# Counting in a routing round: 18 matmuls into [threshold, expert] in place of three with block-diagonal extraction

## The chip, the cores and the metric

The kernel runs on one core of a Trainium2 chip. The metric is the device time of one execution, in microseconds. The profile is that of one execution and comes with its own time.

## What is computed

Three steps follow each other. Attention with queries averaged in pairs gives 2304 rows of 512. A dense layer without a nonlinearity, `((x @ w1) * (x @ w2)) @ w3 @ w_out`, gives new rows of the same shape. Then a mixture of eight experts gives each token to one expert, at most 288 tokens to an expert, in the order of the logits:

```python
    cap = N // E
    logits = x @ w_gate
    order = np.argsort(-logits.flatten())
    for idx in order:
        tok, e = (int(idx) // E, int(idx) % E)
        if assigned[tok] >= 0 or counts[e] >= cap:
            continue
        assigned[tok] = e
        counts[e] += 1
    ...
    for e in range(E):
        mask = assigned == e
        h = np.maximum(x[mask] @ w1[e], 0.0)
        out[mask] = h @ w2[e]
```

## The kernel before

The program is written as a list of operations with costs, dependences and priorities. A planner (`Sched`) simulates the engines with these costs and writes the instructions out in the order of its planned start times. So each engine has one fixed queue in which the stages are interleaved, and the costs that the code states for an operation decide where it stands. Matrix products in float32 are made of three passes, high by high, high by low and low by high part.

The stages in time are: attention (to about 510 us); the hidden layer h, with the logits computed from folded weights beside it (to about 770 us); the product of w3 and w_out, called W, and then x2, the rows that the experts read (to about 953 us); the eight experts (to the end). Routing needs only the logits. Its operations have a smaller priority number than those of W, x2 and the experts, so the planner takes them first where they are ready, and fills the gaps in TensorE's queue with the matmuls of these stages.

Routing replaces the greedy loop by eight phases. Seven of them fix one expert each. In a phase every token that is still free goes to its best open expert (`rt_oh`, one-hot), with its largest logit (`rt_mu`). Then eight rounds search the threshold, four bits at a time, at which the first expert becomes full. A round is a serial chain:

- VectorE compares the logits of 128 x 18 tokens with 15 candidate thresholds (`rt_mask`, [128, 18, 15]).
- TensorE counts in three matmuls of six token groups each, 90 weight columns by 48 moving columns. Only the blocks on the diagonal, where the group of the mask equals the group of the one-hot, mean something.
- VectorE multiplies by a block-diagonal mask (`rt_cnt`), adds the six groups up (`rt_sum`), and spreads the sums over 15 thresholds by 8 experts (`rt_own`, 90 rows of the tile `own8`). A 97th row of `own8` holds minus the free places, `rem`, written once a phase.
- TensorE sums the rows of `own8` with a matrix of ones, so that each partition gets count minus free places.
- VectorE takes the maximum over experts (`rt_any`), compares with zero (`rt_flag`), adds the flags up (`rt_n`), and makes the next base and thresholds of it (`rt_base`, `rt_thr`, `rt_G`).

After the eight rounds a phase assigns its tokens (`rt_ge`, `rt_rows`, a matmul with `rc_neg` and `rc_tri`, `rt_inc` and others). `pick` names the expert that is full, which starts its weight loads by GpSimd's queue, and `slot_lists` makes the list of its tokens with 18 small matmuls (`sl_oh`, `sl_mv`), after which GpSimd gathers their rows. Expert number n can begin when list n is there and x2 is written.

PSUM tiles for routing, the transposes of the gathered rows (`g`) and of the experts' outputs (`ey`) come from the same four slots (`s_pt`). Most operations of these stages are issued through one helper, so the profile gives them all the line L113, and they are told apart by tile. In the rows, u, uh and ul are an expert's weights and their parts, xh, xl and exh, exl the gathered tokens, ehh and ehl the hidden values.

Of the kernel before, what the change touches and what calls it, by code (L numbers as in the profile page):

```python
# [11 lines left out]
F32 = mybir.dt.float32  # L12
F32R = mybir.dt.float32r
BF16 = mybir.dt.bfloat16
F16 = mybir.dt.float16
# [756 lines left out]
NCG = 6  # L772
# [3 lines left out]
def routing_consts(nc, pool, spare):  # L776
# [35 lines left out]

    v = tmp([NCG * NTHR, NCG, 8], F32)
    nc.gpsimd.iota(v, pattern=[[-NTHR, NCG], [0, 8]], base=0, channel_multiplier=1, allow_small_or_imprecise_dtypes=True)
    own = tmp([NCG * NTHR, NCG, 8], F32)
    nc.vector.tensor_scalar(own, v, NTHR - 0.5, None, op0=OP.is_lt)
    c["own"] = diag = pool.tile([NCG * NTHR, NCG, 8], BF16, name="rc_diag")
    nc.vector.scalar_tensor_tensor(diag, v, 0.0, own, op0=OP.is_ge, op1=OP.mult)
    u = tmp([NCG * NTHR, NTHR, NCG], F32)
    nc.gpsimd.iota(u, pattern=[[-1, NTHR], [-NTHR, NCG]], base=0, channel_multiplier=1, allow_small_or_imprecise_dtypes=True)  # L820
    nc.vector.tensor_scalar(u, u, 0.0, None, op0=OP.is_equal)
    c["thr"] = sel = pool.tile([NCG * NTHR, NTHR], F16, name="rc_thr")
    with nc.allow_low_precision(reason="0 or 1"):
        nc.vector.tensor_reduce(sel, u, axis=AX.X, op=OP.max)
    c["ones16"] = ones16 = pool.tile([97, 128], F16, name="rc_ones16")
    nc.vector.memset(ones16, 1.0)

# [25 lines left out]
def routing(nc, sch, rp, slots, c, L, keyL, A, rows_of, idx, prio, prio_l):  # L853
# [11 lines left out]
    r_mx, r_mask = ring("mx", 1, [128, NC], F32), ring("mask", 2, [128, NC, NTHR], BF16)  # L865
    r_flag, r_any, r_n = ring("flag", 2, [128, NTHR], F32), ring("any", 2, [128, NTHR], F32), ring("n", 2, [128, 1], I32)
    r_cnt, r_sum = ring("cnt", 2, [NCG * NTHR, NCG, 8], F16), ring("sum", 2, [NCG * NTHR, 8], F16)
    own8 = rp.tile([97, NTHR, 8], F16, name="rt_own8")
# [17 lines left out]
    dve(120, lambda: nc.vector.memset(own8, 0.0), [], ["own8", "own8r"])  # L886
# [15 lines left out]
    for ph in range(8):  # L902
# [18 lines left out]
        if ph < 7:  # L921

            dve(120, lambda: nc.vector.tensor_scalar(
                own8[96:97], rem[96:97, None, :].to_broadcast([1, NTHR, 8]), 4096.0, -1.0, op0=OP.min, op1=OP.mult), [keyR], ["own8r"])
            base = kb = None
            for rd, b in enumerate(BITS):
# [4 lines left out]
                else:  # L931
# [11 lines left out]
                dve(NC * T, lambda mask=mask, thr=thr, T=T, mu=mu: nc.vector.tensor_tensor(  # L943
                    mask[:, :, :T], mu[:, :, None].to_broadcast([128, NC, T]),
                    thr[:, None, :T].bitcast(F32).to_broadcast([128, NC, T]), op=OP.is_ge), [kmu, kth], [kma])
                ps = Hold(slots)

                def f(ps=ps, mask=mask, oh=oh):
                    for g in range(NC // NCG):
                        gs = slice(g * NCG, g * NCG + NCG)  # L950
                        nc.tensor.matmul(ps.tile[0:NCG * NTHR, 0:NCG * 8], mask[:, gs, :].rearrange("p a t -> p (a t)"),
                                         oh[:, gs, :].rearrange("p a e -> p (a e)"), start=(g == 0), stop=(g == NC // NCG - 1))
                sch.op("PE", 200, f, r=[kma, koh], takes=ps, prio=prio, slack=RT_SLACK)
                (cnt, kc), (sm, ksm), (flag, kf), (any_, kany), (n, kn) = r_cnt(), r_sum(), r_flag(), r_any(), r_n()
                dve(NCG * 8, lambda ps=ps, cnt=cnt: nc.vector.tensor_tensor(
                    cnt.rearrange("p a e -> p (a e)"), ps.tile[0:NCG * NTHR, 0:NCG * 8], c["own"].rearrange("p a e -> p (a e)"), op=OP.mult),
                    [], [kc], uses=[ps])

                def f(cnt=cnt, sm=sm):
                    with nc.allow_low_precision(reason="counts up to 384 are exact"):  # L960
                        nc.vector.tensor_reduce(sm, cnt.rearrange("p a e -> p e a"), axis=AX.X, op=OP.add)
                dve(NCG * 8, f, [kc], [ksm])
                dve(NTHR * 8, lambda sm=sm: nc.vector.tensor_tensor(
                    own8[0:NCG * NTHR], sm[:, None, :].to_broadcast([NCG * NTHR, NTHR, 8]),
                    c["thr"][:, :, None].to_broadcast([NCG * NTHR, NTHR, 8]), op=OP.mult), [ksm], ["own8"])
                ps = Hold(slots)
                sch.op("PE", 110, lambda ps=ps: nc.tensor.matmul(
                    ps.tile[:, 0:NTHR * 8], c["ones16"], own8.rearrange("p t e -> p (t e)"), start=True, stop=True), r=["own8", "own8r"],
                    takes=ps, prio=prio, slack=RT_SLACK)
                dve(NTHR * 8, lambda ps=ps, any_=any_: nc.vector.tensor_reduce(  # L970
                    any_, ps.tile[:, 0:NTHR * 8].rearrange("p (t e) -> p t e", e=8), axis=AX.X, op=OP.max), [], [kany], uses=[ps])
                dve(NTHR, lambda any_=any_, flag=flag: nc.vector.tensor_scalar(flag, any_, 0.0, None, op0=OP.is_ge), [kany], [kf])

                def f(flag=flag, n=n):
# [798 lines left out]
```

## Time and profile before

| | |
|---|---|
| median of three runs | 1259.6 us (1254.34 to 1266.79) |
| the profiled execution | 1264.11 us, of which the span 1262.3 us |
| mean granted TensorE clock | 0.972 |
| TensorE busy | 1175.4 us (93%) |
| VectorE busy | 1037.6 us (82%) |
| GpSimd busy | 692.0 us (55%) |
| ScalarE busy | 640.4 us (51%) |

The span runs from the first to the last instruction. The clock is the share of full speed that TensorE was granted. In rows of groups, the form `out<-in` gives tiles without buffer numbers; the idle time is that of the engine just before these instructions, with what ended it. PE is TensorE, PEld its weight loads, DVE VectorE, ACT ScalarE, POOL GpSimd.

### The profile page before, as it was taken

What the parts mean: (1) busy time and instruction counts of PE and PEld (TensorE: products, weight loads), DVE (VectorE), ACT (ScalarE), POOL (GpSimd) and SP (SyncE); (2) the same over time, 40 slices, a digit from 0 to 9 for tenths busy, and PEclk for the clock granted to TensorE, in tenths of its full rate; (3) what the DMA queues carried; (4) which work ended last, traced back from release to release, by engine and by line L of the source; (5) the groups of instructions that cost most, each with busy time, mean ns of one, the idle gap of its engine ahead of it and who ended that gap; (6) DMA issues with size and microseconds to landing.
All of it is one profiled execution on the core that took longest, in us unless ns stands there. A gap on an engine that the chain in (4) does not pass through costs nothing.

```text
span 1262.3 us, 24072 instructions
## 1 busy us (share of the span) xinstructions
PE 1175.4 (93%) x8377; PEld 1107.6 (88%) x8377; DVE 1037.6 (82%) x2958; ACT 640.4 (51%) x1333; POOL 692.0 (55%) x710
## 2 busy tenths in 40 slices
PE   7999999999999999899999999978898898889995
PEld 5999999999999999899999997756678888789895
DVE  7998999999999999988777876778777998888641
ACT  6888888888888888333222202122222433443330
POOL 4566666666666755455322443264444787767740
PEclk9999999999999999899999999999998999898898
DMA  8676666667666441244555523432223454444530
GB/s 203 157 177 136 156 154 159 153 150 156 153 161 157 115 100 54 68 162 175 174 167 172 180 68 118 158 92 51 63 55 116 158 162 150 148 158 124 186 120 19
DMA packets 116617, 169.87 MB, mean 135 GB/s; under 512 B 47959, under 2 KB 79710, under 8 KB 116494
## 3 DMA queue, kind: packets, MB, share of 16 engines
q1 hardware_dynamic: 104110, 125.33, 38.6%
q0 software_dynamic: 12384, 43.00, 10.5%
q8 instruction: 66, 1.08, 0.4%
q14 instruction: 57, 0.47, 0.1%
HBM read 104.87 MB, written 24.45 MB: 102 GB/s over the span
## 4 chain that ended last, share of the span: by engine, by line
PE 71%; DVE 20%; DMA 3%; issue 2%; POOL 2%; SPq 1%; ACT 1%; POOLq 0%; DVEq 0%; ACTq 0%
PE pb L113 30%; PE s L590 12%; PE pt L614 7%; PE pt L113 6%; PE pt L664 6%; PE s L664 5%; PE s L614 3%; DVE cv_v L113 2%; DVE rt_own L113 2%; DVE rt_flag L113 1%; DVE sl_oh L113 1%; DVE rt_base L113 1%; DMA u<-in_moe_w_dram,rows 1%; DVE rt_mask L113 1%; DVE p L600 1%
## 5 line engine op out<-in xcount | busy, mean ns | idle before, releaser
L600 DVE TENSOR_SCALAR_CACHE_REDUCE p<-s 128x384 f32<-128x384 f32 x432 | 230.2, 551 | 34.9 <-PE pt L614 12.4
L590 PE MATMUL s<-kst,qst 128*128 128x384 f32 x768 | 200.9, 361 | 5.5 <-DVE p L600 5.0
L605 ACT ACTIVATE p<-p,mn 128x1152 f32<-128x1152 f32 x144 | 181.1, 1257 | 23.3 <-DVE mn L603 21.3
L113 PE MATMUL pb<-xhi,wh 128*128 128x288 f32 x512 | 156.7, 306 | 1.7 <-ACT wh L113 1.7
L113 PE MATMUL pb<-xlo,wh 128*128 128x288 f32 x512 | 152.3, 297 | 2.2 <-DVE xlo L113 2.2
L113 PE MATMUL pb<-xhi,wl 128*128 128x288 f32 x512 | 152.2, 297 | 1.1 <-DVE wl L113 1.1
L590 PEld LDWEIGHTS s<-kst,qst 128*128 128x128 f32 x768 | 124.5, 192 | 11.3 <-DVE p L600 9.6
L614 PE MATMUL pt<-ident,p 128*128 128x128 f32 x879 | 132.5, 273 | 0.3 <-ACT p L605 0.3
L648 DVE TENSOR_TENSOR p_lo<-pt,p_hi 128x384 fp32r<-128x384 f32 x230 | 124.5, 551 | 0.7 <-ACT p_hi L331 0.6
L331 ACT ACTIVATE p_hi<-pt 128x384 fp32r<-128x384 f32 x230 | 106.5, 492 | 11.8 <-PE pt L614 11.6
L614 PEld LDWEIGHTS pt<-ident,p 128*128 128x128 f32 x879 | 107.2, 141 | 4.4 <-ACT p L605 0.5
L113 DVE SCALAR_TENSOR_TENSOR cv_v<-cv_raw,cv_v 128x512 int32<-128x512 int32 (+1 forms) x120 | 102.2, 856 | 7.3 <-POOL cv_raw L113 5.1
L113 PEld LDWEIGHTS pb<-xlo,wh 128*128 128x128 f32 x512 | 97.4, 190 | 2.9 <-DVE xlo L113 2.7
L113 PEld LDWEIGHTS pb<-xhi,wh 128*128 128x128 f32 x512 | 97.4, 190 | 2.6 <-ACT wh L113 1.9
L113 PEld LDWEIGHTS pb<-xhi,wl 128*128 128x128 f32 x512 | 97.1, 190 | 1.3 <-DVE wl L113 1.3
L341 POOL TENSOR_TENSOR p_lo<-praw,p_hi 128x384 fp32r<-128x384 f32 x96 | 97.0, 1018 | 0.4
L335 POOL CAST p_hi<-praw 128x384 fp32r<-128x384 f32 x96 | 47.6, 506 | 84.5 <-ACT praw L331 84.5
L113 ACT ACTIVATE a<-pb 128x288 f32<-128x288 f32 x64 | 26.3, 411 | 132.2 <-PE pb L113 123.3
L113 ACT ACTIVATE uh<-u 128x1024 fp32r<-128x1024 f32 (+1 forms) x68 | 57.7, 867 | 66.4 <-DMA u<-in_moe_w_dram,rows 63.6
L113 POOL TENSOR_TENSOR cv_raw<-cv_raw 128x512 f32<-128x512 f32 x40 | 43.2, 1079 | 86.6 <-DVE cv_v L113 67.3
L113 POOL TENSOR_TENSOR ul<-u,uh 128x512 fp32r<-128x512 f32 (+1 forms) x42 | 75.7, 1807 | 25.6 <-ACT uh L113 18.7
L113 POOL DMA_INDIRECT u<-in_moe_w_dram,rows x64 | 69.8, 1090 | 23.8 <-issue 10.3
(317 smaller groups left out, 3497.0 us busy)
## 6 DMA issues: line engine op xcount, KB each, us to landing
cv_raw<-in_moe_w_dram SPq DMA_DIRECT2D x32, 512.0 KB, 4.1
vr<-in_v_dram SPq DMA_DIRECT2D x32, 288.0 KB, 5.3
kr<-in_k_dram SPq DMA_DIRECT2D x32, 288.0 KB, 5.9
kst<-kH SPq DMA_DIRECT2D x31, 288.0 KB, 4.1
kst<-kL SPq DMA_DIRECT2D x31, 288.0 KB, 5.0
qr<-in_q_dram SPq DMA_DIRECT2D x15, 576.0 KB, 6.3
w3t<-wg SPq DMA_DIRECT2D x16, 512.0 KB, 3.7
w<-w3t SPq DMA_DIRECT2D x16, 512.0 KB, 4.2
```

The costliest lines, as they stand in the source:

```text
L113: return f(*[x.get() if isinstance(x, Lazy) else x for x in a], **{n: x.get() if isinstance(x, Lazy) else x for n, x in k.items()})
L331: nc.scalar.activation(out, in_, AF.Copy)
L335: nc.gpsimd.tensor_copy(out, in_)
L341: (nc.vector if eng == "DVE" else nc.gpsimd).tensor_tensor(out, a, b, op=OP.subtract)
L590: nc.tensor.matmul(ps.tile[:, :384], a[:, :], b[:, cs], start=(n == 0), stop=(n == len(passes) - 1))
L600: sch.op("DVE", c_dve(384), lambda ps=ps, c=c, cs=cs: nc.vector.tensor_scalar(t[:, cs], ps.tile[:, :384], 1.0, BIG, op0=OP.mult, op1=OP.mi ...
L605: sch.op("ACT", c_act(S, psum=False, acc=True), lambda: nc.scalar.activation(t, t, AF.Exp, bias=mn[:, 3:4], scale=-1.0, accum_out=sm[0][:, ...
L614: nc.tensor.transpose(ps.tile[:, a * 128:(a + 1) * 128], t[:, b * 128:(b + 1) * 128], ident)
L648: sch.op("DVE", c_dve(384), lambda view=view, src=src: nc.vector.tensor_tensor(view(lo), src(), view(hi).bitcast(F32), op=OP.subtract), us ...
L664: nc.tensor.matmul(ps.tile[:, :n], vt[:, t, :, :], src[half][:, t, off:off + n], start=(half == 0 and t == 0), stop=(half == 1 and t == NT ...
```

## The change

The count is made straight into [threshold, expert]. For each of the 18 token groups one matmul takes 15 columns of the mask, widened to 128 weight columns, and the 8 columns of the one-hot, and all 18 add up in PSUM. Rows 0 to 14 of the result are counts; the others hold sums of neighbouring columns that nobody reads. The mask tile becomes flat, 17 x 15 + 128 wide, and its last columns are cleared once. VectorE compares the counts with the free places directly out of PSUM into `rt_flag` ([15, 8] of a tile of 128 rows, the rest cleared once). A matmul with ones adds the flags over thresholds, and VectorE takes the maximum over experts as `rt_n`. The tiles `rt_cnt`, `rt_sum`, `own8` and `rt_any` and their constants go, as does the copy of the free places into `own8` in each phase. The costs that the planner gets change with them: 500 ns for the 18 matmuls in place of 200, 60 in place of 110 for the sum.

```diff
-NCG = 6
+MW = 17 * NTHR + 128
...
-    c["own"] = diag = pool.tile([NCG * NTHR, NCG, 8], BF16, name="rc_diag")
...
-    c["thr"] = sel = pool.tile([NCG * NTHR, NTHR], F16, name="rc_thr")
...
-    c["ones16"] = ones16 = pool.tile([97, 128], F16, name="rc_ones16")
...
-    dve(120, lambda: nc.vector.memset(own8, 0.0), [], ["own8", "own8r"])
+    for _ in range(2):
+
+        (flag, kf), (mask, kma) = r_flag(), r_mask()
+        dve(8, lambda flag=flag: nc.vector.memset(flag, 0.0), [], [kf])
+        dve(128, lambda mask=mask: nc.vector.memset(mask[:, NC * NTHR:MW], 0.0), [], [kma])
...
-            dve(120, lambda: nc.vector.tensor_scalar(
-                own8[96:97], rem[96:97, None, :].to_broadcast([1, NTHR, 8]), 4096.0, -1.0, op0=OP.min, op1=OP.mult), [keyR], ["own8r"])
...
                 ps = Hold(slots)
 
                 def f(ps=ps, mask=mask, oh=oh):
-                    for g in range(NC // NCG):
-                        gs = slice(g * NCG, g * NCG + NCG)
-                        nc.tensor.matmul(ps.tile[0:NCG * NTHR, 0:NCG * 8], mask[:, gs, :].rearrange("p a t -> p (a t)"),
-                                         oh[:, gs, :].rearrange("p a e -> p (a e)"), start=(g == 0), stop=(g == NC // NCG - 1))
-                sch.op("PE", 200, f, r=[kma, koh], takes=ps, prio=prio, slack=RT_SLACK)
...
+                    for g in range(NC):
+                        nc.tensor.matmul(ps.tile[:, 0:8], mask[:, g * NTHR:g * NTHR + 128], oh[:, g, :], start=(g == 0), stop=(g == NC - 1))
+                sch.op("PE", 500, f, r=[kma, koh], takes=ps, prio=prio, slack=RT_SLACK)
+                (flag, kf), (n, kn) = r_flag(), r_n()
+                dve(8, lambda ps=ps, flag=flag: nc.vector.tensor_tensor(
+                    flag[0:NTHR, :], ps.tile[0:NTHR, 0:8], rem[0:NTHR, :], op=OP.is_ge), [keyR], [kf], uses=[ps])
+
                 ps = Hold(slots)
-                sch.op("PE", 110, lambda ps=ps: nc.tensor.matmul(
-                    ps.tile[:, 0:NTHR * 8], c["ones16"], own8.rearrange("p t e -> p (t e)"), start=True, stop=True), r=["own8", "own8r"],
-                    takes=ps, prio=prio, slack=RT_SLACK)
-                dve(NTHR * 8, lambda ps=ps, any_=any_: nc.vector.tensor_reduce(
-                    any_, ps.tile[:, 0:NTHR * 8].rearrange("p (t e) -> p t e", e=8), axis=AX.X, op=OP.max), [], [kany], uses=[ps])
-                dve(NTHR, lambda any_=any_, flag=flag: nc.vector.tensor_scalar(flag, any_, 0.0, None, op0=OP.is_ge), [kany], [kf])
...
+                sch.op("PE", 60, lambda ps=ps, flag=flag: nc.tensor.matmul(
+                    ps.tile[:, 0:8], c["ones"], flag, start=True, stop=True), r=[kf], takes=ps, prio=prio, slack=RT_SLACK)
+
+                def f(ps=ps, n=n):
                     with nc.allow_low_precision(reason="a count up to 15"):
-                        nc.vector.tensor_reduce(n, flag, axis=AX.X, op=OP.add)
-                dve(NTHR, f, [kf], [kn])
+                        nc.vector.tensor_reduce(n, ps.tile[:, 0:8], axis=AX.X, op=OP.max)
+                dve(8, f, [], [kn], uses=[ps])
```

## Rows read from the trace of the kernel before

**Rows 1.** Page, chain that ended last, by engine.

```profile
PE 71%; DVE 20%; DMA 3%; issue 2%; POOL 2%; SPq 1%; ACT 1%; POOLq 0%; DVEq 0%; ACTq 0%
```

**Rows 2.** Stretches by stage; us, busy per engine, clock, DMA, GB/s.

```profile
773.00:953.00 180.00, 157.53 (x830) 120.53 (x829) 134.84 (x464) 45.56 (x79) 78.28 (x68) 0.97 0.31 86
953.00:1138.00 185.00, 158.56 (x1211) 152.87 (x1210) 162.69 (x475) 68.24 (x127) 132.14 (x121) 0.93 0.47 150
1138.00:1262.00 124.00, 104.14 (x776) 102.52 (x775) 64.43 (x128) 34.61 (x65) 65.17 (x67) 0.91 0.36 114
```

**Rows 3.** TensorE groups, 777 to 950 us; busy, mean ns, idle before.

```profile
L113 PE MATMUL pt<-rt_oh,rt_mask 128*90 128x48 bf16 x96 | 9.2, 201 | 15.9 <-DVE rt_mask L113 9.5 <-DVE rt_oh L113 6.4
...
L113 PE MATMUL pt<-rt_own,rc_ones 97*128 97x120 f16 x32 | 7.3, 228 | 3.7 <-DVE rt_own L113 3.5
...
L113 PE MATMUL pt<-rt_rows,rc_neg 128*128 128x8 bf16 x6 | 0.6, 166 | 1.4 <-DVE rt_rows L113 1.4
```

**Rows 4.** Groups of TensorE, 950 to 1160 us.

```profile
L113 PE MATMUL pt<-ident,g 96*128 96x96 f32 x66 | 8.1, 260 | 4.2 <-DVE rt_al L113 2.7 <-DVE exl L113 1.1 <-DVE rt_any L113 0.4
...
L113 PE MATMUL pt<-rt_oh,rt_mask 128*90 128x48 bf16 x72 | 6.8, 201 | 11.8 <-DVE rt_mask L113 7.7 <-DVE rt_oh L113 3.8 <-DVE exl L113 0.4
...
L113 PE MATMUL pt<-rt_own,rc_ones 97*128 97x120 f16 x24 | 5.6, 233 | 6.2 <-DVE rt_own L113 5.1 <-DVE sl_fl L113 1.0
```

**Rows 5.** Groups of VectorE, 770 to 1135 us.

```profile
L113 DVE TENSOR_TENSOR rt_own<-rt_sum,rc_thr 90x120 f16<-90x120 f16 x56 | 29.1, 519 | 1.6
...
L113 DVE TENSOR_SCALAR rt_flag<-rt_any 128x15 f32<-128x15 f32 x56 | 25.0, 446 | 1.5
...
L113 DVE TENSOR_REDUCE rt_any<-pt 128x15 f32<-128x120 f32 x56 | 15.7, 280 | 27.4 <-PE pt L113 27.4
...
L113 DVE TENSOR_REDUCE rt_sum<-rt_cnt 90x8 f16<-90x48 f16 x56 | 13.1, 233 | 1.4
...
L113 DVE TENSOR_TENSOR rt_cnt<-pt,rc_diag 90x48 f16<-90x48 f32 x56 | 11.2, 200 | 21.7 <-PE pt L113 21.4
...
L113 DVE TENSOR_REDUCE rt_n<-rt_flag 128x1 int32<-128x15 f32 x56 | 9.4, 168 | 1.6
...
L113 DVE TENSOR_TENSOR rt_r<-pt,rt_rem 128x8 f32<-128x8 f32 x6 | 1.0, 158 | 0.0
```

**Rows 6.** Tiles rt_own and rt_flag; ns minimum/median/maximum.

```profile
L113 DVE TENSOR_TENSOR rt_own<-rt_sum,rc_thr x56: 253/280/2355, 781.5 to 1126.4; 90x120 f16<-90x120 f16 x56
...
L113 DVE TENSOR_SCALAR rt_flag<-rt_any x56: 151/175/2914, 783.7 to 1128.0; 128x15 f32<-128x15 f32 x56
```

**Rows 7.** Timeline of one round; start, us, engine.

```profile
849.61 0.43 DVE L113 TENSOR_TENSOR rt_mask<-rt_mu,rt_thr 128x270 bf16<-128x270 f32 x1
...
850.32 0.27 PE L113 MATMUL pt<-rt_oh,rt_mask 128*90 128x48 bf16 x3
...
850.43 0.48 PE L113 MATMUL pb<-Wl,x2h 128*128 128x512 f32 x1
...
853.23 0.43 DVE L113 TENSOR_TENSOR rt_mask<-rt_mu,rt_thr 128x270 bf16<-128x270 f32 x1
```

**Rows 8.** TensorE timeline, three matmuls with 128-column weights.

```profile
815.32 0.19 PE L113 MATMUL pt<-rt_rows,rc_neg 128*128 128x8 bf16 x2 [0.71 <-DVE rt_rows L113]
815.37 0.17 PE L113 MATMUL pt<-rt_rows,rc_tri 128*128 128x8 bf16 x1
815.40 0.47 PE L113 MATMUL pb<-wo,w 128*128 128x512 f32 x1
```

**Rows 9.** TensorE timeline, a slot list's 18 matmuls.

```profile
1156.86 0.95 PE L113 MATMUL pt<-sl_mv,sl_oh 128*96 128x6 bf16 x18 [0.92 <-POOL sl_mv L113]
1157.66 0.39 PE L113 MATMUL pb<-exh,uh 128*128 128x288 f32 x1
```

**Rows 10.** TensorE timeline, first matmuls of the seventh and eighth expert.

```profile
1191.97 0.39 PE L113 MATMUL pb<-exh,uh 128*128 128x288 f32 x1
...
1221.80 0.39 PE L113 MATMUL pb<-exh,uh 128*128 128x288 f32 x1
```

More of the change, by code (lines that the diff above doesn't have):

```diff
@@ L811, in routing_consts @@
     c["grid"] = grid
[L813 to L816, printed above, removed]
-    c["own"] = diag = pool.tile([NCG * NTHR, NCG, 8], BF16, name="rc_diag")
[L818 to L821, printed above, removed]
-    c["thr"] = sel = pool.tile([NCG * NTHR, NTHR], F16, name="rc_thr")
-    with nc.allow_low_precision(reason="0 or 1"):
-        nc.vector.tensor_reduce(sel, u, axis=AX.X, op=OP.max)
-    c["ones16"] = ones16 = pool.tile([97, 128], F16, name="rc_ones16")
-    nc.vector.memset(ones16, 1.0)
     t0 = pool.tile([128, NTHR], I32, name="rc_t0")
@@ L864, in routing @@
     r_t8, r_oh = ring("t8", 2, [128, NC, 8], F32), ring("oh", 2, [128, NC, 8], BF16)
[L865 to L868, printed above, removed]
+    r_mx, r_mask = ring("mx", 1, [128, NC], F32), ring("mask", 2, [128, MW], BF16)
+    r_flag, r_n = ring("flag", 2, [128, 8], BF16), ring("n", 2, [128, 1], I32)
     r_base, r_thr, r_G = ring("base", 2, [128, 1], I32), ring("thr", 2, [128, NTHR], I32), ring("G", 2, [128, NTHR], I32)
@@ L942, in routing @@
                             G, c["grid"][rd + 1][0], base, None, op0=OP.bitwise_xor), [kb], [kG])
-                dve(NC * T, lambda mask=mask, thr=thr, T=T, mu=mu: nc.vector.tensor_tensor(
-                    mask[:, :, :T], mu[:, :, None].to_broadcast([128, NC, T]),
-                    thr[:, None, :T].bitcast(F32).to_broadcast([128, NC, T]), op=OP.is_ge), [kmu, kth], [kma])
+                dve(NC * T, lambda mask=mask, thr=thr, mu=mu: nc.vector.tensor_tensor(
+                    mask[:, 0:NC * NTHR].rearrange("p (c t) -> p c t", t=NTHR), mu[:, :, None].to_broadcast([128, NC, NTHR]),
+                    thr[:, None, :].bitcast(F32).to_broadcast([128, NC, NTHR]), op=OP.is_ge), [kmu, kth], [kma])
@@ L954, in routing @@
[L954 to L965, printed above, removed]
-                ps = Hold(slots)
-                sch.op("PE", 110, lambda ps=ps: nc.tensor.matmul(
-                    ps.tile[:, 0:NTHR * 8], c["ones16"], own8.rearrange("p t e -> p (t e)"), start=True, stop=True), r=["own8", "own8r"],
-                    takes=ps, prio=prio, slack=RT_SLACK)
@@ L970, in routing @@
-                dve(NTHR * 8, lambda ps=ps, any_=any_: nc.vector.tensor_reduce(
-                    any_, ps.tile[:, 0:NTHR * 8].rearrange("p (t e) -> p t e", e=8), axis=AX.X, op=OP.max), [], [kany], uses=[ps])
-                dve(NTHR, lambda any_=any_, flag=flag: nc.vector.tensor_scalar(flag, any_, 0.0, None, op0=OP.is_ge), [kany], [kf])
-                def f(flag=flag, n=n):
+                    for g in range(NC):
+                        nc.tensor.matmul(ps.tile[:, 0:8], mask[:, g * NTHR:g * NTHR + 128], oh[:, g, :], start=(g == 0), stop=(g == NC - 1))
```

## The prediction

> **What bounds the kernel now.** I read the page first, then the busy time by stage, then the waits of TensorE inside the stages that hold routing, and last the timeline of single rounds. The chain that ended last lies 71% on TensorE and 20% on VectorE [rows 1]. So a TensorE microsecond added is nearly a microsecond of time, and a VectorE microsecond saved is worth only what TensorE waits for it. Routing runs in two stages [rows 2]: from 773 to 953 us beside the matmuls that make x2, and from 953 to 1138 us beside the first experts. TensorE is busy 157.5 of 180 us in the one and 158.6 of 185 us in the other; VectorE 134.8 and 162.7, so in the second stage it is the more loaded of the two. The granted clock falls from 0.97 to 0.93 and 0.91. Work lost to it is one minus the clock, times the stage: 5, 13 and 11 us.
>
> The reader is to see in [rows 3, 4] why TensorE, with other work at hand, stands still at all. Its queue is in order, and a routing matmul sits in it where the planner expected its data. When VectorE is late, everything behind waits. 32 rounds (96 matmuls in threes) lie before 950 us and 24 after. The waits inside rounds, for rt_mask and rt_own, are 9.5 + 3.5 us before 950 and 7.7 + 5.1 after: 25.8 us. The waits between phases, for rt_oh, rt_rows and, on the transposes of g, rt_al, are 6.4 + 1.4 us for four phases before 950 and 3.8 + 2.7 after.
>
> Why VectorE is late: rt_own takes 519 ns on the mean but 280 at the median, and up to 2355; rt_flag 446 against 175, up to 2914 [rows 5, 6]. Their excess over the median is 56 x (0.239 + 0.271) = 28.6 us. rt_sum, rt_cnt, rt_any and rt_n have means near what one such instruction needs (233, 200, 280, 168 ns) and no such tail in the timelines I read. So the tail belongs to the form of the two instructions, which read only SBUF and are not reductions, and not to VectorE being full.
>
> **The change part by part.** *TensorE.* Three matmuls of 48 columns become 18 of 8 columns, each with its own weight load of 128 columns. The three cost 850.32 to 850.43, 0.11 us, before the next matmul starts [rows 7]. For the 18 there are two rows. Three bf16 matmuls of 8 columns with 128-column weights (rc_neg twice, rc_tri once) went from 815.32 to 815.40, 27 ns each [rows 8]. The 18 matmuls of a slot list, 6 columns with 96-column weights, went from 1156.86 to 1157.66, 44 ns each [rows 9]. I take 27, because width and type are the same: 18 x 0.027 = 0.48, so +0.37 us a round and 56 x 0.37 = +20.7 us. The upper end is 44 ns scaled from 96 to 128 columns, 59 ns: +0.95 a round, +53 us; at 44 as it stands +0.68, +38 us. Below 27 no row reaches. What no row shows is a weight load that begins at an odd element, as every second slice of the new mask does (steps of 15), so the upper end stays open. The matmul that sums stays one per round and only gets narrower: nothing.
>
> The Trainium skill, TensorE: Matmul & The Clock Gate, section LDWEIGHTS, gives a load as its columns over 1.2 GHz, an estimate of 107 ns for 128, which would make the 18 cost 1.9 us and the change some +100 us. The trace speaks against that reading: 27 ns a pair. The same page, Weight-path perf modes, says that 128 weights of a type other than FP32 load on a faster path, and that agrees with 27 against 44 ns; it says nothing of odd starts.
>
> *VectorE.* A round loses rt_cnt, rt_sum, rt_own, rt_any and rt_flag as they are and gets a flag from PSUM and rem, in the form of rt_r (158 ns), and a maximum out of PSUM that I price as rt_n (168 ns). Removed is 56 x (0.200 + 0.233 + 0.519 + 0.280 + 0.446 + 0.168) = 103.4 us, added 56 x 0.326 = 18.3: 85 us less [rows 5]. On the chain of one round the first half is 0.95 - 0.16 = 0.79 us shorter, the second 0.89 - 0.17 = 0.72, and the count 0.37 longer: 1.15 us with the tails, 0.64 without. The round in [rows 7], mask to mask, took 853.23 - 849.61 = 3.62 us; it should take some 2.7. Both new instructions read at most one operand from SBUF, or are reductions, so I expect no tail on them.
>
> *What the shorter round is worth.* Inside rounds, the two instructions with the tail go, while rt_base, rt_thr, rt_G and rt_mask, which read SBUF alone, stay and may take over part of it. I keep 40% of the 25.8 us (between 30% and 80%): -15.5 us. Between phases nothing in the code changes but one copy of rem, and the waits per phase stay; but with shorter rounds about a phase and a half more is done before x2 ends, where a phase costs (6.4 + 1.4) / 4 = 2.0 us, and fewer wait in the expert stage, where 3.8 + 2.7 fall away: +3 - 6.5, about -4. Where TensorE no longer stands, the clock does not fall behind the stall: of the 13 us lost in the second stage and the part of the 11 that lies before 1160, I take 10 back (between 3 and 15). With 85 us less, VectorE is sooner at the other work that TensorE waits for, the 1.1 us on exl and the like: -2. And the last lists are ready earlier, which takes a wait at the end of routing, bounded by 0 and 4: -2.
>
> *The rest.* The constants and own8's clearing that go lie in the first microseconds and in one place before the first round, the new clearing of mask and flag is a few hundred ns under the other work of VectorE at 777 us: nothing. What moves is the plan: the planner holds 500 ns for the 18 matmuls, near my 0.48, and 2 VectorE entries in place of 6, so all work after 777 us is put in another order. The gathers, weight loads and scatters on GpSimd's queue stay the same in number.
>
> The sum, against the profiled execution's own 1264.1 us: 20.7 - 15.5 - 4 - 10 - 2 - 2 = -12.8, so 1251. That execution is 4.5 us over the median of the three runs, so against 1259.6 the same sum gives 1247, and I set 1246, since the sum leaves the constants out.
>
> **The rivals.** *More gain.* An expert without routing beside it took 1191.97 to 1221.80, 29.8 us [rows 10]. Eight at that pace are 239 us, and from 953 us to the end of the span there are 309 [rows 2]. If shorter rounds put nearly all of routing in front of the experts, and I leave 28 us for the first gathers, the last scatters and the rounds left, 42 us are in reach. The x2 stage pays +12: 44 rounds in place of 32, each 0.37 dearer (+16) and the twelve new ones with their old price (+4), less 8 of waits. That is -30: 1234 against the profiled execution, 1230 against the median. For it: VectorE's 162.7 of 185 us; against it: phase ends and lists still run there.
>
> *No change.* The waits do not go but move from rt_own to the flag and from one SBUF instruction to the next. With 80% of the 25.8 us kept and 3 us of clock back: 20.7 - 5 - 4 - 3 - 2 - 2 = +5, with the new order as noise, 1256 to 1272 against the median, about 1264. For it: rt_mask's wait has the larger share, and mask stays as it is.
>
> *Slower.* The weight load at an odd start does not run at 27 ns. It decides from 27 + 12.8 / (56 x 18) us = 40 ns a matmul. At 44 the sum is +4 and the longer round gives back half of the 15.5: 1271; at 59 it is +20 and all of it goes back: 1295. I price it at 1278. For it: the queue of 18 stands in front of x2's matmuls, on the engine that binds.
>
> *That it does not do what it says*: if the plan put the rounds no closer together, the mask-to-mask time would stay near 3.6 us; that is within "no change".
>
> **How the numbers follow.** Forecast -13: 0.38; more gain 0.22; no change 0.22; slower 0.18. A measurement of this kernel tells about 1%, 12.6 us, from nothing. Faster by over that (below 1247) takes the 0.22 and a little over half of the forecast: 0.44. Slower (above 1272): 0.18 and an edge of no change, 0.19. The rest, 0.37, is within. The range takes in more gain down to 1226 and slower up to 1278, which leaves about 0.1 out on each side.
>
> **What would show it.** In the changed kernel's profile: 18 matmuls from rt_mask start to the next matmul in about 0.48 us, even and odd slices alike; a flag near 160 ns with no tail; mask to mask about 2.7 us where nothing else is queued; the idle time before the mask matmuls and the flag's matmul about 10 us in place of 25.8; four phases done well before 953 us; the x2 stage ending up to 12 us later and the expert stage over 20 us shorter, at a clock above 0.93. Wrong would be: 40 ns or more a matmul, waits inside rounds above 20 us, or an expert stage that stays at its length because something else than VectorE sets it.

## The result and the profile after

The changed kernel takes 1275.6 us (median of eight runs, 1272.3 to 1278.2) where the kernel before, beside it, takes 1260.5 (1254.3 to 1269.6): ratio 1.0112, interval 1.0076 to 1.0148. It is slower by 1.1%. Forecast was 1246, a gain; the time lies inside the range, but the kernel became slower. The profiled execution took 1278.2 us, span 1276.3, granted clock 0.973. Against [rows 1] the chain that ended last lies less on TensorE and VectorE (68% and 16%, from 71% and 20%) and more on transfers and GpSimd (5% each, from 3% and 2%). First its shares by engine, then by line, in the page of the changed kernel:

```profile
PE 68%; DVE 16%; DMA 5%; POOL 5%; issue 4%; ACT 1%; SPq 0%; POOLq 0%; DVEq 0%; ACTq 0%
PE pb L113 27%; PE s L590 12%; PE pt L614 7%; PE pt L113 6%; PE pt L664 6%; PE s L664 5%; DMA u<-in_moe_w_dram,rows 4%; PE s L614 3%; DVE cv_v L113 2%; POOL u L113 2%; POOL ul L113 1%; DVE rt_base L113 1%; DVE p L600 1%; DVE ul L113 1%; POOL g L113 1%
```

A load of expert weights (u<-in_moe_w_dram,rows) now holds 4% of it. The same stretches as in [rows 2], after (the columns are us, busy of PE, PEld, DVE, ACT and POOL, clock, DMA share, GB/s). Behind them come five slices of 10 us, then the two stages cut where x2 ends, and then both as one:

```profile
773.00:953.00 180.00, 159.99 (x1352) 117.58 (x1350) 117.83 (x431) 38.38 (x66) 71.20 (x66) 0.92 0.29 79
953.00:1138.00 185.00, 165.25 (x1424) 156.05 (x1425) 122.11 (x324) 61.45 (x115) 114.54 (x111) 0.94 0.47 142
1138.00:1276.00 138.00, 117.82 (x889) 115.77 (x887) 65.82 (x103) 39.51 (x79) 71.53 (x72) 0.95 0.40 126
...
830.00:840.00 10.00, 6.28 (x60) 4.30 (x59) 6.26 (x11) 3.01 (x5) 5.94 (x6) 0.95 0.35 113
840.00:850.00 10.00, 7.25 (x28) 5.34 (x28) 8.72 (x21) 3.31 (x6) 5.55 (x5) 0.84 0.23 67
850.00:860.00 10.00, 8.95 (x73) 6.70 (x73) 8.76 (x32) 1.14 (x3) 5.36 (x7) 0.69 0.06 13
860.00:870.00 10.00, 7.53 (x62) 5.32 (x62) 5.64 (x18) 2.28 (x5) 4.39 (x4) 0.83 0.37 93
...
1000.00:1010.00 10.00, 8.17 (x86) 7.53 (x86) 4.00 (x20) 1.09 (x3) 4.88 (x5) 0.66 0.22 56
...
773.00:999.70 226.70, 202.89 (x1815) 154.16 (x1814) 150.84 (x566) 47.22 (x83) 87.80 (x83) 0.92 0.28 75
999.70:1276.00 276.30, 240.17 (x1850) 235.25 (x1848) 154.93 (x292) 92.13 (x176) 169.47 (x164) 0.94 0.47 148
773.00:1276.00 503.00, 443.06 (x3663) 389.41 (x3661) 305.77 (x857) 139.35 (x259) 257.27 (x247) 0.94 0.38 115
```

The same view of the kernel before: two slices, the two stages cut where its x2 ends, and both as one:

```profile
860.00:870.00 10.00, 8.15 (x38) 6.14 (x37) 8.94 (x29) 2.87 (x5) 4.37 (x4) 1.00 0.27 63
870.00:880.00 10.00, 8.30 (x56) 6.36 (x55) 8.99 (x35) 2.06 (x4) 4.51 (x5) 1.00 0.25 57
...
773.00:959.80 186.80, 164.32 (x889) 127.24 (x888) 141.47 (x497) 46.86 (x82) 80.51 (x71) 0.97 0.31 86
959.80:1262.00 302.20, 255.90 (x1927) 248.68 (x1925) 220.49 (x568) 101.56 (x187) 195.08 (x186) 0.92 0.43 137
773.00:1262.00 489.00, 420.22 (x2813) 375.92 (x2811) 361.96 (x1063) 148.41 (x269) 275.59 (x256) 0.94 0.38 118
```

So the first stage lasts 226.7 us in place of 186.8, +39.9, and the experts 276.3 in place of 302.2, -25.9. In the first stage TensorE is busy 38.6 us more and stands 1.3 us more (23.8 against 22.5). One minus the clock, times the stage, is 18.1 us against 5.6: 12.5 of the 38.6. The rest, 26 us, is work: 52 rounds lie there (936 small matmuls) in place of 33, all at the new price. Over both stages together TensorE is busy 22.8 us more and stands 8.9 us less (59.9 against 68.8), at a mean clock of 0.94 in either kernel.

A round, the longest stall of the first stage, and a wait between experts, in the timeline of the changed kernel (start, us, engine; in brackets the idle time before, and what ended it):

```profile
792.44 0.43 DVE L113 TENSOR_TENSOR rt_mask<-rt_mu,rt_thr 128x270 bf16<-128x270 f32 x1
...
793.17 0.61 PE L113 MATMUL pt<-rt_oh,rt_mask 128*128 128x8 bf16 x18
...
793.63 0.93 PE L113 MATMUL pb<-wo,w 128*128 128x512 f32 x3
...
795.18 0.43 DVE L113 TENSOR_TENSOR rt_mask<-rt_mu,rt_thr 128x270 bf16<-128x270 f32 x1
...
833.26 4.28 DVE L113 SCALAR_TENSOR_TENSOR rt_base<-rt_n,rt_base 128x1 int32<-128x1 int32 x1
833.81 2.50 POOL L113 TENSOR_TENSOR ul<-u,uh 128x512 fp32r<-128x512 f32 x2
...
836.26 1.26 POOL L113 TENSOR_TENSOR Wl<-wt,Wh 128x512 fp32r<-128x512 f32 x1
...
838.21 0.61 PE L113 MATMUL pt<-rt_oh,rt_mask 128*128 128x8 bf16 x18 [3.72 <-DVE rt_mask L113]
...
1087.35 3.32 DVE L113 CAST uh<-u 128x1024 fp32r<-128x1024 f32 x1 [5.62 <-DMA u<-in_moe_w_dram,rows]
1087.76 2.35 POOL L113 TENSOR_TENSOR ul<-u,uh 128x1024 fp32r<-128x1024 f32 x1
1090.59 0.44 DVE L113 SCALAR_TENSOR_TENSOR ehl<-pb,ehh 128x288 fp32r<-128x288 f32 x1
...
1091.09 0.41 PE L113 MATMUL pb<-exh,uh 128*128 128x288 f32 x1 [3.90 <-DVE ehl L113]
```

The 18 matmuls take 793.17 to 793.63, 0.46 us, 26 ns each, odd starts included. Mask to mask is 795.18 - 792.44 = 2.74 us, against 3.62 in [rows 7]. At 833.26 an instruction on one element a partition takes 4.28 us: it ends, at 837.54, 0.02 us after GpSimd's row of three elementwise operations (833.81 to 837.52). `rt_thr` and `rt_mask` follow, and the matmuls that wait for the mask start at 838.21, before which TensorE has stood 3.72 us. At 1087.35 VectorE has waited 5.62 us for a weight load, converts it in 3.32 us beside GpSimd's `ul`, and only then makes `ehl`, for which TensorE stands 3.90 us.

What TensorE waits for from 770 to 1300 us, by groups of the changed kernel (busy us, mean ns, idle just before; the last three rows are VectorE's, `rt_base` from 770 to 1150 us and the conversions of weights from 770 to 1300):

```profile
L113 PE MATMUL pb<-exh,uh 128*128 128x288 f32 x244 | 77.0, 315 | 6.3 <-DVE ehl L113 6.3
...
L113 PE MATMUL pb<-ehl,uh 128*128 128x288 f32 x256 | 75.6, 295 | 1.3 <-DVE ehl L113 1.2
...
L113 PE MATMUL pt<-rt_oh,rt_mask 128*128 128x8 bf16 x1008 | 34.3, 167 | 23.0 <-DVE rt_mask L113 11.9 <-DVE rt_oh L113 11.0
L113 PE MATMUL pt<-ident,ey 128*96 128x128 f32 x96 | 14.2, 292 | 7.6 <-DVE ey L113 4.5 <-ACT ey L113 3.0
L113 PE MATMUL pt<-rt_flag,rc_ones 128*128 128x8 bf16 x56 | 10.3, 184 | 2.0 <-DVE rt_flag L113 2.0
...
L113 DVE SCALAR_TENSOR_TENSOR rt_base<-rt_n,rt_base 128x1 int32<-128x1 int32 x49 | 18.9, 385 | 1.6
...
L113 DVE CAST uh<-u 128x1024 fp32r<-128x1024 f32 x9 | 14.8, 1648 | 13.3 <-DMA u<-in_moe_w_dram,rows 13.3
L113 DVE CAST uh<-u 128x512 fp32r<-128x512 f32 x12 | 7.0, 586 | 11.1 <-DMA u<-in_moe_w_dram,rows 11.1
```

The kernel before in the same view, but for the routing rows, which [rows 3, 4] have:

```profile
L113 PE MATMUL pb<-ehl,uh 128*128 128x288 f32 x256 | 77.7, 304 | 1.7 <-DVE ehl L113 1.7
...
L113 PE MATMUL pt<-ident,ey 128*96 128x128 f32 x96 | 14.5, 304 | 2.6 <-DVE ey L113 2.6
...
L113 DVE CAST uh<-u 128x1024 fp32r<-128x1024 f32 x6 | 12.1, 2013 | 7.4 <-DMA u<-in_moe_w_dram,rows 7.4
```

Waits inside rounds are 11.9 + 2.0 = 13.9 us, from 25.8. Waits for `ehl` and `ey` are 15.0 (3.0 of them for an `ey` of ScalarE), from 4.3, and VectorE itself stands 24.4 us ahead of conversions of weights that have not landed, from 7.9. Single tiles of the changed kernel (minimum/median/maximum ns, first and last start in us):

```profile
L113 DVE TENSOR_TENSOR rt_flag<-pt,rt_rem x56: 144/154/156, 783.4 to 1012.6; 15x8 bf16<-15x8 f32 x56
...
L113 DVE TENSOR_REDUCE rt_n<-pt x56: 147/167/168, 784.2 to 1013.6; 128x1 int32<-128x8 f32 x56
L113 DVE SCALAR_TENSOR_TENSOR rt_base<-rt_n,rt_base x49: 152/160/4284, 789.4 to 1013.8; 128x1 int32<-128x1 int32 x49
...
L113 PE MATMUL pb<-Wh,x2h x168: 277/393/777, 838.7 to 999.6; 128*128 128x512 f32 x120, 128*128 128x256 f32 x48
```

The two new VectorE instructions have no tail. `rt_base`, which had some of it before (mean 290 ns, up to 2144), now has more: mean 385, up to 4284. Routing's last round is at 1012.6, where [rows 6] has 1126.4 and 1128.0 for its tiles.

### The profile page after: what moved, and what is told of

Its sections match the earlier page's. It is cut to its first block, busy times and chain, and to the rows that moved or that the text cites. A ratio compares the mean times of both kernels' runs of the same rounds, so it can differ in the third digit from the quotient of the medians.

```text
span 1276.3 us, 25493 instructions
## 1 busy us (share of the span) xinstructions
PE 1192.7 (93%) x9217; PEld 1114.8 (87%) x9217; DVE 980.1 (77%) x2745; ACT 630.2 (49%) x1322; POOL 672.6 (53%) x699
## 4 chain that ended last, share of the span: by engine, by line
PE 68%; DVE 16%; DMA 5%; POOL 5%; issue 4%; ACT 1%; SPq 0%; POOLq 0%; DVEq 0%; ACTq 0%
PE pb L113 27%; PE s L590 12%; PE pt L614 7%; PE pt L113 6%; PE pt L664 6%; PE s L664 5%; DMA u<-in_moe_w_dram,rows 4%; PE s L614 3%; DVE cv_v L113 2%; POOL u L113 2%; POOL ul L113 1%; DVE rt_base L113 1%; DVE p L600 1%; DVE ul L113 1%; POOL g L113 1%
## 5 line engine op out<-in xcount | busy, mean ns | idle before, releaser
L600 DVE TENSOR_SCALAR_CACHE_REDUCE p<-s 128x384 f32<-128x384 f32 x432 | 230.0, 551 | 38.6 <-PE s L590 14.8
L331 ACT ACTIVATE p_hi<-pt 128x384 fp32r<-128x384 f32 x230 | 106.4, 492 | 11.9 <-PE pt L614 11.7
L113 ACT ACTIVATE uh<-u 128x1024 fp32r<-128x1024 f32 (+1 forms) x63 | 53.8, 867 | 84.2 <-DMA u<-in_moe_w_dram,rows 84.1
L113 POOL TENSOR_TENSOR x2l<-hraw,x2h 128x512 fp32r<-128x512 f32 x36 | 48.9, 1361 | 77.6 <-ACT x2h L113 70.8
```

Of the source, the lines that this page charges most:

```text
L113: return f(*[x.get() if isinstance(x, Lazy) else x for x in a], **{n: x.get() if isinstance(x, Lazy) else x for n, x in k.items()})
L331: nc.scalar.activation(out, in_, AF.Copy)
L600: sch.op("DVE", c_dve(384), lambda ps=ps, c=c, cs=cs: nc.vector.tensor_scalar(t[:, cs], ps.tile[:, :384], 1.0, BIG, op0=OP.mult, op1=OP.mi ...
```

## The experiments

All ratios are to the kernel before, on the same chip. The theory that the runs were made to try: the change pays some 20 us on TensorE, gets back what its shorter rounds save in waits, and loses the rest to two things that it brings forward, stalls of VectorE next to GpSimd beside x2, and experts that run ahead of their weights. The rivals: the small matmuls cost more than their time (through the clock), or the rounds are only packed too densely.

**The price alone.** The kernel before, with 15 more matmuls of the new kind in each round, into columns that nobody reads:

```diff
+                    flat = mask.rearrange("p c t -> p (c t)")
+                    for g in range(15):
+                        nc.tensor.matmul(ps.tile[:, 64:72], flat[:, 9 * g:9 * g + 128], oh[:, g, :], start=(g == 0), stop=(g == 14))
-                sch.op("PE", 200, f, r=[kma, koh], takes=ps, prio=prio, slack=RT_SLACK)
+                sch.op("PE", 600, f, r=[kma, koh], takes=ps, prio=prio, slack=RT_SLACK)
```

> The kernel before with 15 more matmuls of 8 columns per round, with 128-column weights out of the mask, into PSUM columns that nobody reads; the planner holds 600 ns for the group. The time on TensorE is 15 x 0.026 = 0.39 us a round more, 22 us in all. Theory price (the count on TensorE is paid one for one, since TensorE binds): +15 to +25 us against the kernel before, so 1276 to 1286, with the waits inside rounds near the 25.8 us of before. Rival cover (the matmuls hide in TensorE's waits, and the loss of the change lies in the order that the shorter rounds give): within 6 us of the kernel before.

1.0184 (1.0146 to 1.0222): 23 us, between 18 and 28, where 22 is one for one. So TensorE pays for them in full; the waits inside rounds give back little of it (10.1 us for `rt_mask` and 11.1 for `rt_own`, 21.2 in place of 25.8).

**The 18 matmuls twice**, the second time into PSUM columns 8 to 15, planned at 970 ns:

```diff
+                    for g in range(NC):
+                        nc.tensor.matmul(ps.tile[:, 8:16], mask[:, g * NTHR:g * NTHR + 128], oh[:, g, :], start=(g == 0), stop=(g == NC - 1))
-                sch.op("PE", 500, f, r=[kma, koh], takes=ps, prio=prio, slack=RT_SLACK)
+                sch.op("PE", 970, f, r=[kma, koh], takes=ps, prio=prio, slack=RT_SLACK)
```

> The changed kernel with the 18 matmuls made twice, the second time into PSUM columns that nobody reads; the planner holds 970 ns. 0.47 us a round more, 26 us in all. Price: +20 to +28 us against the changed kernel, so 1296 to 1304. Cover: under +8. Theory clock (small matmuls next to a wait let the granted clock fall): the clock in the stage of x2 falls below the 0.92 of the changed kernel and the time rises by more than 28.

1.0212 (1.0161 to 1.0264), 1.0% over the changed kernel at the medians, less than the price of 26 us. Its four executions spread from 1282.9 to 1296.4 us, and the profiled one is the longest. Two stretches of it, and both stages as one:

```profile
773.00:953.00 180.00, 167.51 (x1989) 129.17 (x1988) 104.65 (x408) 36.88 (x64) 67.72 (x63) 0.96 0.29 80
953.00:1138.00 185.00, 168.43 (x1703) 158.74 (x1703) 118.86 (x336) 54.30 (x103) 111.43 (x108) 0.91 0.44 128
...
773.00:1294.00 521.00, 468.38 (x4686) 417.97 (x4684) 298.17 (x857) 137.98 (x258) 262.49 (x250) 0.94 0.38 112
```

With 36 small matmuls a round the clock is 0.96 beside x2, above the changed kernel's 0.92, and 0.91 from 953 to 1138 us, below its 0.94. Over both stages it is 0.94, as in the changed kernel and in the kernel before. So nothing here shows that small matmuls lower the clock, and that rival falls. Doubling gave back part of its price in waits (`rt_mask` and `rt_oh` 14.7 us in place of 22.9).

**More room in the plan.** RT_SLACK is how long after its operands the planner places a routing matmul. 450, 200 and 700 ns in place of 0, 300 ns in the kernel before, and 800 on the 18 matmuls alone or 900 on the sum alone:

```diff
-LIST_SLACK, RT_SLACK = 0.0, 0.0
+LIST_SLACK, RT_SLACK = 0.0, 450.0
```

> The changed kernel with RT_SLACK 450 in place of 0: the planner puts each of a round's two matmul groups 450 ns later, so a planned round is as long as before the change, while the data are there earlier. Theory density (packing all rounds beside x2 and the missing slack cost the stalls and the clock of that stage): the waits for rt_mask and rt_flag fall from 14 us to under 4, the clock from 773 to 953 us returns to 0.97, some 33 rounds before 953, and the time comes to 1255 to 1266. Rival price: TensorE's extra 20 us stay whatever the order, and what routing leaves the x2 stage it costs the experts: 1270 to 1278.

> The same with RT_SLACK 200. Density: between, 1262 to 1270, with waits inside rounds of some 6 us. Price: 1270 to 1278.

> The kernel before with RT_SLACK 300 on both matmul groups of a round. Theory slack helps either kernel (the plan holds no time for the tails of VectorE, so TensorE's queue comes to a routing matmul too early): the waits inside rounds fall from 25.8 us to some 12 and the time by 5 to 12 us, to 1249 to 1256. Rival, slack is what the change took away (the old round held enough of it): within 4 us of the kernel before, or slower, because the last lists come later.

> The changed kernel with a slack of 800 ns on the 18 matmuls alone, ahead of which the tails of rt_base and rt_mask lie, and none on the matmul that sums. The planned round is as long as with twice 450, less 100 ns. Theory waits (what counts is that TensorE does not come to the mask too early): 1253 to 1261, the wait for rt_mask under 5 us. Theory density (what counts is how many rounds lie beside x2): as with twice 450, 1256 to 1262.

> The changed kernel with a slack of 900 ns on the matmul that sums and none on the 18: the planned round is exactly as long as with twice 450, so the rounds are as dense, but the time is held where no tail lies. Density: 1256 to 1262 as with twice 450. Waits: the wait for rt_mask stays near the changed kernel's 11.9 us and the time near 1266 to 1274.

> The changed kernel with RT_SLACK 700 on both. Waits: those inside rounds fall under 6 us, but the last rounds come later, into the experts: 1254 to 1262. If routing's end becomes the bound (the last list after the seventh expert's start), over 1264.

| | ratio | interval |
|---|---|---|
| slack 450 | 0.9988 | 0.9966 to 1.0010 |
| slack 200 | 1.0031 | 1.0003 to 1.0058 |
| before, slack 300 | 1.0001 | 0.9978 to 1.0024 |
| 800 on the 18 alone | 1.0024 | 1.0002 to 1.0046 |
| 900 on the sum alone | 1.0102 | 1.0059 to 1.0145 |
| slack 700 | 1.0077 | 1.0049 to 1.0105 |

Room of 450 undoes the loss of the changed kernel, and 300 does nothing for the kernel before. With 450 on both and 900 on the sum the plan stretches a round by the same 900 ns, and 34 and 33 rounds lie before 953 us in place of 40; the one gains 1.2% and the other nothing. So thinner packing alone does not bring the time back. It does help beside x2 in either (with 900 on the sum TensorE is busy 165.1 of 180 us there, at a clock of 0.96), but that run loses as much beside the experts (152.4 of 185 us, where the changed kernel has 165.3). The sum with 900 still waits at the 18 matmuls (rows of the mask matmul, 770 to 1300 us, for 800 on the 18 and then for 900 on the sum):

```profile
L113 PE MATMUL pt<-rt_oh,rt_mask 128*128 128x8 bf16 x1008 | 34.3, 167 | 13.9 <-DVE rt_mask L113 7.4 <-DVE rt_oh L113 4.7 <-DVE exl L113 1.0
```

```profile
L113 PE MATMUL pt<-rt_oh,rt_mask 128*128 128x8 bf16 x1008 | 33.9, 167 | 25.9 <-DVE rt_oh L113 12.1 <-DVE rt_mask L113 11.6 <-DVE sl_pre L113 0.9
```

Room in front of the 18, behind `rt_base`, `rt_thr` and `rt_mask`, where the tail now sits, is worth more than room in front of the sum (1.0024 against 1.0102), though the wait then moves in part to `rt_flag` (16.2 us, from 2.0). At 700, waits for `ehl` and `rt_flag` (7.9 and 9.8 us) take the place of those taken away.

**Less of GpSimd beside x2, and weights planned as late as they land.** The low parts of x2's operands (x2l) on VectorE, and the planner told 5200 ns for a load of weights in place of 3500 (issue to landing is 5.2 us at the median in the changed kernel's transfers, 4.7 before). The changed kernel's row, with name, queue, count and median us:

```profile
u<-in_moe_w_dram,rows POOLq DMA_INDIRECT x64, 5.2
```

Each alone, with slack, and later in the kernel before and both together:

```diff
-        xs[t], xo[t] = x2_split(t, pr, ("POOL",)), r_xo()
+        xs[t], xo[t] = x2_split(t, pr, ("DVE",)), r_xo()
...
-            r=[("rows_of", n)], w=[("ur", c)] + free, prio=pr, lat=3500)
+            r=[("rows_of", n)], w=[("ur", c)] + free, prio=pr, lat=5200)
```

> The changed kernel with the low parts of x2's rows (x2l) made by VectorE in place of GpSimd; 36 splits of some 0.55 us move, about 20 us of VectorE, which is busy 118 of 180 us there. Theory tails (what delays the rounds is VectorE's instructions with only SBUF operands waiting for GpSimd's long ones): from 777 to 953 us the mean of rt_base falls from its 385 ns towards 200, the wait for rt_mask there from 8.6 us to under 4, the clock above 0.94, the time by 6 to 15 us: ratio to the kernel before 0.999 to 1.006. Rival, VectorE's queue is what delays them: the waits stay or grow, ratio 1.010 or more.

> The same with RT_SLACK 450. If tails and missing slack are the same cost, the two do not add up: ratio 0.996 to 1.001. If they are two, 0.988 to 0.995.

> The changed kernel with 5200 ns in place of 3500 as the planner's time from an expert's weight load to its landing; 5.2 us is what the trace shows. Theory weights (with routing done early, the experts' stage waits through VectorE's queue for weights that the plan believes to be there): the waits of TensorE for ehl and ey, 15 us in the changed kernel, fall under 6 us, the time by 5 to 10 us, ratio 1.003 to 1.007. Rival (those waits are GpSimd's blocking of VectorE, not the landing): ratio 1.008 to 1.014, waits as they are.

> RT_SLACK 450 and 5200 ns together, the candidate for a version better than both. Where the waits for ehl and ey are small already (4 us with 450 alone), little is left: ratio 0.994 to 1.000.

> The kernel before with 5200 ns as the planner's landing time of the weights. Theory new wait (the experts wait for weights only since routing is done early; before, TensorE's waits for ehl and ey are some 4 us): ratio 0.996 to 1.004. Rival, the plan was wrong for both alike: 0.980 to 0.990.

> The kernel before with x2l made by VectorE. If the tails cost both kernels (before the change rt_own and rt_flag carry them): waits inside rounds before 953 us from 13 to some 6 us, ratio 0.988 to 0.996. If they came to matter only with the change, or VectorE, busy 135 of 180 us there, becomes the bound: 0.997 to 1.006.

> The changed kernel with both edits. If the two losses are separate they add up: ratio 0.972 to 0.982. If either only moves the wait into the other: 0.986 to 0.994.

> The kernel before with both edits. Theory: without the price of 20 us but with the long rounds beside the experts, 0.988 to 0.998, so the changed kernel with both is the faster. Rival: 0.970 to 0.982, and the change loses to it by its price.

| | changed kernel | kernel before |
|---|---|---|
| as it is | 1.0112 (1.0076 to 1.0148) | 1 |
| x2l on VectorE | 0.9943 (0.9920 to 0.9966) | 0.9913 (0.9886 to 0.9940) |
| load planned at 5200 ns | 0.9900 (0.9854 to 0.9946) | 0.9945 (0.9924 to 0.9966) |
| both | 0.9861 (0.9829 to 0.9893) | 0.9801 (0.9759 to 0.9844) |
| x2l and slack 450 | 0.9917 (0.9884 to 0.9951) | |
| 5200 and slack 450 | 0.9983 (0.9958 to 1.0008) | |

Each setting alone helps both kernels, the changed one more: 1.7% against 0.9% for x2l, 2.1% against 0.55% for the load. Together they give 2.5% against 2.0%, and that difference is not clear of the intervals. The changed kernel is 1.1% behind as it is and 0.6% with both, so at the medians the two account for about half of its loss, and that half is itself within the intervals. Slack on top of x2l adds 0.3%, inside the intervals: these two mostly recover the same loss.

With x2l moved, the first stage of the changed kernel by stretches, the group of its mask matmul from 777 to 950 us, and its `rt_base` from 770 to 1150:

```profile
773.00:953.00 180.00, 172.14 (x1537) 131.29 (x1535) 127.64 (x507) 44.95 (x78) 35.55 (x40) 0.97 0.32 87
```

```profile
L113 PE MATMUL pt<-rt_oh,rt_mask 128*128 128x8 bf16 x756 | 25.5, 167 | 7.8 <-DVE rt_mask L113 4.9 <-DVE rt_oh L113 2.9
...
L113 DVE SCALAR_TENSOR_TENSOR rt_base<-rt_n,rt_base 128x1 int32<-128x1 int32 x49 | 14.9, 303 | 1.5
```

GpSimd has half the work, TensorE is busy 12 us more of the same stretch, the clock is 0.97, and x2 ends 30 us sooner (969.8). 42 rounds (756 matmuls) lie before 950 us, where the changed kernel as it is has 40, with 18.0 us of idle time ahead of the mask matmuls. But the tail of `rt_base` is only shorter (mean 303 from 385 ns, still up to 4290 in one instance). The edit also makes x2l itself faster (a median of 0.69 us on VectorE, 1.29 on GpSimd) and gives the plan another order, so how much of the 1.7% comes from the stalls beside GpSimd is not settled. Beside the experts the waits for `ehl` and `ey` grow, to 19.4 us.

With the later load, from 770 to 1300 us:

```profile
L113 PE MATMUL pb<-ehh,uh 128*128 128x288 f32 x256 | 77.3, 302 | 1.7 <-DVE ehl L113 1.7
...
L113 PE MATMUL pb<-exh,uh 128*128 128x288 f32 x244 | 75.2, 308 | 0.5 <-DVE ehl L113 0.5
...
L113 PE MATMUL pt<-ident,ey 128*96 128x128 f32 x96 | 12.2, 273 | 0.7 <-DVE ey L113 0.6
```

Of the 15.0 us 2.9 are left, and VectorE stands 8.4 us ahead of conversions in place of 24.4: the planner less often puts the conversion of a load that has not landed ahead of `ehl` in VectorE's queue. These 12 us are 1.0% of the time; what the rest of the 2.1% is was not found. The pairing with slack was meant to be better than both and was not: 5200 with 450 (0.9983) is worse than 5200 alone and no better than 450 alone (0.9988), with clock 0.89 from 953 to 1138 us. Why, is not settled.

With both, the kernel before is the fastest run of all, 1234.0 us, and the changed kernel takes 1241.4; the intervals overlap a little. What TensorE waits for inside rounds there, changed kernel and then kernel before, 770 to 1300 us:

```profile
L113 PE MATMUL pt<-rt_oh,rt_mask 128*128 128x8 bf16 x1008 | 34.0, 167 | 9.0 <-DVE rt_oh L113 4.7 <-DVE rt_mask L113 4.0 <-DVE exl L113 0.2
```

```profile
L113 PE MATMUL pt<-rt_oh,rt_mask 128*90 128x48 bf16 x168 | 15.9, 201 | 13.9 <-DVE rt_mask L113 8.6 <-DVE rt_oh L113 5.3
...
L113 PE MATMUL pt<-rt_own,rc_ones 97*128 97x120 f16 x56 | 12.8, 229 | 10.5 <-DVE rt_own L113 10.5
```

The waits inside rounds are 4.0 us there in place of 8.6 + 10.5 = 19.1, so 15.1 less, and TensorE stands 58.4 us of the whole span in place of 72.5. The clock of the whole execution is the same (medians 0.9805 and 0.980).

**The price again, without these losses**, and **fewer rounds.** The 15 matmuls of the first experiment in the kernel before with both settings; and the changed kernel with both, searching five bits a round (31 thresholds, 49 rounds in all in place of 56; its mask has one buffer, and the last, narrower round its own flag tile):

```diff
-BITS = (4,) * 8
+BITS = (5,) * 6 + (2,)
```

> The kernel before with both edits and the 15 additional small matmuls per round of the first experiment. Theory (price one for one, and the shorter rounds give back about 13 us): 15 to 23 us over the kernel before with both edits, ratio 0.992 to 0.999, so 8 to 16 us over the changed kernel with both. Rival (with the tails gone there is room for the matmuls): ratio under 0.988.

> The changed kernel with both edits and thresholds of five bits: 31 of the 128 weight columns are used in place of 15, a phase has seven rounds in place of eight (six of five bits, one of two). 49 groups of 18 matmuls in place of 56; the mask is 558 columns and some 0.29 us longer in six rounds of a phase. Price theory: 7 x 0.65 = 4.5 us less on TensorE and a chain of a phase about 1 us shorter: ratio 0.980 to 0.985. Rival (the longer masks on VectorE eat it): 0.986 to 0.992.

The first: 0.9990 (0.9976 to 1.0003), that is 0.0189 or 24 us (18 to 30) over the same kernel without them. The second: 0.9825 (0.9807 to 0.9842), 0.4% under the changed kernel with both, with intervals that overlap. With both settings, the price is 24 us and the changed kernel stands 0.0129, 16 us (12 to 21), below before plus price: that is what shorter rounds give back here.

Not all expectations came true. x2l and the later load gained more in the changed kernel than either of their cases said; the matmuls made twice and the later load in the kernel before came out between their cases; both settings in the changed kernel did not add up, as its second case has it; 800 on the 18 alone was a little slower than both of its cases; for slack in the kernel before, and for both settings in it, the rival came true; and with slack 450 the waits inside rounds fell to 9.1 us, not under 4.

## Why the prediction was wrong

Right: *18 matmuls in 0.48 us* (0.46), *mask to mask 2.7* (2.74), *a flag near 160 ns with no tail* (154, at most 156), *over 20 us less in the experts* (25.9). *+20.7 on TensorE*: 23 (18 to 28) and 24 (18 to 30) measured. *Phase ends -4*: `rt_oh` 11.0 and `rt_rows` 0.6 us, from 10.2 and 2.7, and 2.7 for `rt_al` that are gone, make -4.0. The rival *slower* named the wrong mechanism: odd starts cost nothing that shows. The range reaches up to the measured time for its sake, so that the time lies inside is luck.

*Waits inside rounds -15.5*: -11.9, a little small, for the reason that the prediction gave as possible. Part of the tail moved to the next instruction that reads only SBUF: `rt_base`, 385 ns on the mean (290 before) against 160 at the median. VectorE's busy time fell by 57.5 us (1037.6 to 980.1), not 85.

The steps that failed are two. *Clock -10.* By the three stretches after, one minus the clock is 14.4 + 11.1 + 6.9 = 32 us, against 29 before: +3. By the clock of the profiled executions (0.973 and 0.972) it is 34.5 against 35.3, and by the rows from 773 us on 0.94 in both. So nothing came back that can be told from noise; the four executions of the price alone differ by 0.970 to 0.980. The prediction looked for a gain behind 953 us and left out the first stage, where 52 rounds now lie: by the stretches 6 us do come back behind 953, and 9 more are lost ahead of it. With both settings TensorE stands 14.1 us less than in the kernel before with the same settings, and the clock is still the same (0.9805 and 0.980). So less standing did not bring clock with it there, though the two settings themselves went with a better clock in either kernel (0.9735 and 0.977 without them). What standing is worth in clock stays open; that the change brought none of the 10 us does not.

Why the first stage lost clock is open. The total of standing is nearly the same there (23.8 and 22.5 us), but not its distribution: before, two slices in a row with 1.9 and 1.7 us of idle time run at 1.00; after, 3.7 and 2.8 us of idle time in two slices stand ahead of 0.69 and 0.83. That bunched stalls cost the clock would be a reading of these slices. The slice from 1000 us, at 0.66 with 1.8 us of idle time, does not fit it, and no run isolates it.

*The x2 stage pays +12*, said of the rival with more gain, was +39.9. Its work came to 26 us in place of 20, with 52 rounds in place of 44; the 8 us of waits that it was to save did not go (+1.3); and 12.5 us of clock were put at nothing.

*VectorE sooner at the other work -2.* Waits for `ehl` and `ey` went from 4.3 to 15.0 us, +10.7. Routing out of the way lets the experts reach their weights sooner than these land, and VectorE, in order, stands at the conversion (24.4 us in place of 7.9) with TensorE's next operand behind it. The prediction looked for a new wait inside routing alone; none of its cases had this one. In the run with the later load 2.9 of the 15.0 us are left.

*The last lists -2* is not to be seen. The terms as measured are 23 - 11.9 - 4.0 + 3 + 10.7 = +21 us, against +14.0 of the spans; by TensorE's rows from 773 us on, busy +22.8 and standing -8.9. The terms are 7 us too many: each is from one trace, and some overlap. Put together, the forecast took 33.5 us back from its price; the changed kernel as it is gets back about 8 (a price of 23, a loss of 15), and 16 where both settings are in.

Would the change win without the two losses? No run says so: with both settings it is behind by 0.6% at the medians, at best level. Its price is paid whole on the engine that binds, and 16 us come back. What stays open: settings of the plan move either kernel by about 1% and don't add (both settings give the kernel before 2.0% where each gives 0.9 and 0.55, and the changed kernel 2.5% where each gives 1.7 and 2.1), so parts under half a per cent are not to be assigned.

## What to carry to other kernels

Where work is moved onto the engine that binds, count its price in full, as it was paid here, and the waits that it is to take away only in part; set the price against the waits that the same rows show as removable, and count what becomes early, not only what becomes short. A stage that is freed can run into the next resource's landing time, so check how the planned latency of its loads stands to the measured one. Try the cheaper edit first: here two settings gave the kernel before 2.0%.

## What the runs showed of the hardware that was not expected

Weight loads of 128 bf16 columns that begin at an odd element were no slower: 18 matmuls, every second with an odd start, took 0.46 us, 26 ns each, where three whose weights are whole tiles took 27 each [rows 8]. A VectorE instruction of one element a partition that reads and writes only SBUF (`rt_base`) took up to 4284 ns, and in that instance ended 0.02 us after a row of three GpSimd operations, while comparison and maximum out of PSUM stayed within 144 to 168 ns over 112 instances. Twice as many small matmuls left the granted clock from 773 us to the end at 0.94, and 14.1 us less standing of TensorE, with both settings, left that of the whole execution at 0.98.
